# Attention and two feed-forward layers on one core: weights held split, six blocks of 384 tokens, attention's output stored as addends

## The chip, the core and the metric

The kernel runs on 1 core of a Trainium2 chip (8 cores; the other seven idle). The metric is the device time of one execution in microseconds (us), lower being better. TensorE is called PE here, VectorE DVE, ScalarE ACT, GpSimd POOL and SyncE SP. The kernel's DMAs are issued by SP, a few of them by ACT or POOL; an engine's DMA queue has a q behind its name (SPq, ACTq).

## The reference

Attention over 4 batches of 8 heads, 576 tokens and 64 columns a head, with rotary embedding; its output is x with 2304 tokens of 512 columns. Then two feed-forward layers ("MoE" in the names, but with one expert), from 512 to 2048 and back. q, k and v are float32; the weights are float64 and reach the kernel as pairs of 32-bit words, which it has to convert itself.

```python
q_rot, k_rot = rotate(q), rotate(k)
scores = scale * np.matmul(q_rot, k_rot.transpose(0, 1, 3, 2))
scores = scores - np.max(scores, axis=-1, keepdims=True)
attn = np.exp(scores)
attn = attn / (np.sum(attn, axis=-1, keepdims=True) + 1e-09)
x = np.matmul(attn, v)               # then to [2304, 512]
h = np.maximum(x @ w_in, 0.0)
x = h * h @ w_out                    # layer 0
h = x @ w_in2
g = np.maximum(h, 0.0) + alpha * np.minimum(h, 0.0)
out = g @ w_out2                     # layer 1
```

## The kernel before, in words

**Precision.** PE multiplies in fp32r, which keeps fewer bits than float32. Each factor is therefore split into a high part (a copy to fp32r) and a low part (the factor less its high part), and each product is three matmuls: high × high, high × low, low × high. A matmul here has a 128 × 128 stationary tile and streams up to 512 columns.

**Attention** (`attention`, L49) takes two heads at a time, 16 pairs. A pair has nine steps. `scores` (L190) does four or eight 288-column matmuls into PSUM, the row maximum on DVE (L208) and the exponential on ACT, which also sums the rows (L209). `trans` (L217) and `trans_tail` (L234), four steps later, transpose the exponentials on PE and split them on the way out of PSUM (L214 on ACT, L215 on DVE). `pv` (L250) multiplies with v in ten matmuls per half head. In a tile of `pv`, rows 0 to 63 belong to the high part of v and rows 64 to 127 to the low part, and the two halves have still to be added. `copy` (L125) brings it to SBUF as `st`. `outp` (L263) transposes `st` back (L280, L285: ten transposes a pair), adds the two halves (ACT L290, DVE L291) and multiplies by the reciprocal of the row sums on POOL (L292) into xn. After the four pairs of a batch, `xturn` (L294) transposes xn again (L300, 20 transposes a batch) and sends x to DRAM (L306). `turn` (L142) transposes the rotated q and k of the next pair, splits them (L148, L149) and stacks the parts by 18 DMAs on SP (L179). The rotary embedding (`rope`) runs on POOL.

Through attention the order on every engine is chosen by the framework's scheduler, which lets ready instructions pass others. After it, `manual_schedule` (L568) makes PE, DVE, ACT and POOL take program order.

**MoE** (`moe`, L396) has five blocks of tokens (`BLOCKS`, L388: 512, 256, 512, 512, 512). A layer takes block after block, and in each block 16 units of the first product (z = 0) and 16 of the second (z = 1). One unit uses one weight of 128 × 512 and has 12 matmuls. In layer 1's second product the weights are the streamed side, 512 columns for each 128 tokens. For a weight, `convert` (L421) loads the 64-bit words (L425) and takes them apart on DVE (L431 to L433), `power` (L436) forms the exponent on ACT, and `join` (L440) puts the sign in on DVE (L442) and multiplies mantissa and power on POOL (L444). The float32 weights are held. At each use, `prepare` (L460) splits the weight again with `split` (L447): the high part on ACT (L451), the low part on DVE or POOL (L452). That makes 320 splits. `prepare_x` (L468) loads a chunk of 128 columns of x for a block and splits it; `finish` (L509) applies the activation, in layer 0 a relu on ACT (L516) and the square on POOL (L525), or at the block's end copies the result out. The table `jobs` (L548) says ahead of which unit each weight is converted: layer 0's weights one a unit during the first block, layer 1's during the last block of layer 0 and the first of layer 1.

Of the kernel before, what the change touches and what calls it, by code (L numbers as in the profile page):

```python
# [9 lines left out]
F32 = mybir.dt.float32  # L10
# [17 lines left out]
NQ = 5  # L28
# [5 lines left out]
KQB, STB, XNB, PTB = 2, 4, 1, 3  # L34
RB = 2
# [3 lines left out]
XOE, STE = "A", "AAAA"  # L39
OP, OPD, OO, OX, OXD, OV = 0, 2, 3, 6, 2, 3  # L40


def col_base(b):

    g = (b // 2) * 2 * S
    return (g, g + 512) if b % 2 == 0 else (g + 640, g + 576)


def attention(tc, q, k, v, ident, ident_d, rope_d, xd, follow):  # L49
# [8 lines left out]
    with ExitStack() as at:  # L58
# [5 lines left out]
        sm = pool("asm", 2)  # L64
        kq = fpool("akq", KQB)
        nat = fpool("anat", 1)
        rp = fpool("arope", 1)
        ld = fpool("ald", 2)
        cp = fpool("acst", 1)
        ps_sc = fpool("ps_sc", NSC, space=PSUM)  # L70
# [13 lines left out]
        raw, rot = {}, {}  # L84

        def load(n, nm, heads=slice(0, 2), tail=None):
            b, hp = pairs[n]
            src = k if nm == "k" else q
            if (n, nm) not in raw:
                raw[n, nm] = ld.tile([P, 2, 5, D], F32, name=f"{nm}raw")  # L90
            m = raw[n, nm]
            hs = slice(2 * hp + heads.start, 2 * hp + heads.stop)
            nc.sync.dma_start(out=m[:, heads, 0:4].rearrange("p h r d -> p h (r d)"),
                              in_=src[b, hs, 0:512, :].rearrange("h (p r) d -> p h (r d)", r=4))
            for x in range(2):
                (tail or nc.sync).dma_start(out=m[64 * x:64 * x + 64, heads, 4],
                                            in_=src[b, hs, 512:576, :].rearrange("h p d -> p h d"))

        def load_v(n):
            b, hp = pairs[n]  # L100
            hs = slice(2 * hp, 2 * hp + 2)
            m = ld.tile([P, 2, NQ, D], F32, name="vraw")
            nc.sync.dma_start(out=m[:, :, 0:4].rearrange("p h r d -> p h (r d)"),
                              in_=v[b, hs, 0:512, :].rearrange("h (p r) d -> p h (r d)", r=4))
            for j in range(2):
                nc.sync.dma_start(out=m[64 * j:64 * j + 64, j, 4], in_=v[b, 2 * hp + j, 512:576, :])
                G.memset(m[64 - 64 * j:128 - 64 * j, j, 4], 0.0)
            raw[n, "v"] = m

        def rope(n, nm, c0=0, c1=NR, E=G):  # L110
            w = c1 - c0
            x = raw[n, nm].rearrange("p h r (t d) -> p (h r) t d", t=2)[:, c0:c1]
# [12 lines left out]
        def copy(out, in_, e):  # L125
            if e == "A":
                A.activation(out=out, in_=in_, func=AF.Copy)
            else:
                V.tensor_copy(out=out, in_=in_)

        vv, ops = {}, {}

        def vsplit(n):

            x = raw[n, "v"].rearrange("p h r d -> p (h r) d")
            t = sm.tile([P, 2, NQ, 2, D], F32R, name="vs", bufs=KQB)
# [51 lines left out]
        sums, Pt, PT, xn = {}, {}, {}, {}  # L188

        def scores(n, i, j):  # L190
            qT, kH, kL = ops[n]
            if (i, j) == (0, 0):
                sums[n] = sm.tile([P, 9], F32, name="sums", bufs=3)
# [8 lines left out]
            for y, (lhs, k0) in enumerate(prods):  # L202
                for kx, st in ((kH, True), (kL, False)):
                    for hf in range(2):
                        T.matmul(sc[:, hf, 0:SH], lhsT=lhs, rhs=kx[:, k0 + hf * SH:k0 + (hf + 1) * SH],  # L205
                                 start=st and y == 0, stop=not st and y == len(prods) - 1)
# [3 lines left out]
                         func=AF.Exp, bias=nm, accum_out=sums[n][:, 2 * i + j:2 * i + j + 1])  # L210
# [38 lines left out]

        def pv(n, j, hf, st):  # L250
# [3 lines left out]
            for c in range(NQ):  # L254
                for x in range(2):
                    t = PT[n, j][x][:, c, sl] if c < 4 else PT[n, "tail"][x][:, sl]
                    T.matmul(acc[:, 0:SH], lhsT=vs[:, j, c].rearrange("p a d -> p (a d)"), rhs=t,  # L257
                             start=(c == 0 and x == 0), stop=(c == 4 and x == 1))
            copy(st[:, sl], acc[:, 0:SH], STE[2 * j + hf])

        ris = {}

        def outp(n, j, sts):  # L263

            b, hp = pairs[n]
            if (hp, j) == (0, 0):
                xn[b] = sm.tile([P, NQ, DM], F32, name="xn", bufs=XNB)
            if j == 0:
                s, ri = sums[n], sm.tile([P, NQ, 2], F32, name="ri", bufs=3)
                rf = ri.rearrange("p i j -> p (i j)")  # L270
                V.tensor_scalar(s, s, 1e-9, None, ALU.add)
                V.reciprocal(rf[:, 0:9], s)
                V.tensor_copy(out=rf[0:64, 9:10], in_=rf[64:128, 8:9])
                ris[n] = ri
            ri = ris[n]
            u = ps_t.tile([P, 512], F32, name="ps", tag="t")
            if j < 2:
                rows, w, h = P, 4, 2 * hp + j
                for i in range(4):
# [363 lines left out]
```

## Time and profile before

| what | value |
|---|---|
| median of 3 runs | 1238.13 us (1237.96 to 1240.72) |
| profiled execution | 1237.75 us |
| its span, first to last instruction | 1235.9 us |
| mean granted TensorE clock | 0.992 of full speed |
| DMA traffic | 103.43 MB, mean 84 GB/s |
| busy: PE, DVE, ACT, POOL | 1131.9, 889.6, 706.6, 546.7 us |

A row of a view gives for each instruction group its line of the kernel (L205), its engine and operation, and the tiles it writes and reads (out<-in). What stands in brackets at a row's end is the idle time in front of it and what ended it. Busy times of different engines overlap; only a wait that ends last costs time. The kernel has stages one after the other (attention, layer 0, layer 1), and a mean over the span mixes them, so the table of stretches tells more than the shares of the whole.

### The profile page before, as it was taken

Reading aid. Unit: us, or ns where it says so; the run is one execution under the profiler, and the core shown is the slowest. Engines: PE = TensorE matmul, PEld = TensorE weight load, DVE = VectorE, ACT = ScalarE, POOL = GpSimd, SP = SyncE. Lnnn points to the kernel's source line nnn. Section 1 sums busy time; section 2 is a strip of 40 time slices with the busy share of each in tenths; the row PEclk is TensorE's granted clock in tenths of the full one; section 3 lists DMA queues with packets and bytes.
Section 4 is the critical chain, followed back from the end, with each engine's and each line's share of the span. In section 5 each row is a group of like instructions: output and inputs, shape, how many; then the busy total and the mean of one; then the engine's idle time right before and its main releaser. Section 6 shows DMA issues by size and latency. Waiting matters only on the chain.

```text
span 1235.9 us, 17781 instructions
## 1 busy us (share of the span) xinstructions
PE 1131.9 (92%) x6096; PEld 960.4 (78%) x6096; DVE 889.6 (72%) x1353; ACT 706.6 (57%) x1470; POOL 546.7 (44%) x493
## 2 busy tenths in 40 slices
PE   2799999999988766999999999998899999999998
PEld 1698989898876544898888887776689888888887
DVE  3688878788799999474544569999978665465453
ACT  1588888888875544574544454554456545445443
POOL 7667665764225465403104026556536250340430
PEclk9899999999999999999999999999999999999999
DMA  6656665756545434210010123342210101000100
GB/s 162 157 126 163 146 165 132 167 136 126 135 124 171 126 113 135 69 53 1 26 43 1 34 69 110 102 134 69 81 61 15 45 1 35 34 1 10 35 1 34
DMA packets 93496, 103.43 MB, mean 84 GB/s; under 512 B 29664, under 2 KB 68576, under 8 KB 93408
## 3 DMA queue, kind: packets, MB, share of 16 engines
q1 hardware_dynamic: 92720, 101.63, 30.7%
q8 instruction: 48, 0.79, 0.3%
q10 hardware_dynamic: 432, 0.56, 0.1%
q14 instruction: 40, 0.33, 0.1%
q0 software_dynamic: 256, 0.13, 0.0%
HBM read 58.76 MB, written 14.16 MB: 59 GB/s over the span
## 4 chain that ended last, share of the span: by engine, by line
PE 67%; DVE 12%; issue 7%; ACT 4%; POOL 4%; SPq 3%; DMA 2%; ACTq 0%; DVEq 0%; POOLq 0%
PE py L507 27%; PE ph L490 8%; PE ph L488 8%; PE ph L489 8%; PE sc L205 5%; PE acc L257 4%; PE ps L226 4%; ACT p L209 2%; SPq L179 2%; POOL w L444 2%; DVE pw L442 2%; DVE wl L452 2%; DVE man L433 2%; POOL wl L452 2%; DVE nm L208 1%
## 5 line engine op out<-in xcount | busy, mean ns | idle before, releaser
L452 DVE TENSOR_TENSOR wl<-w,wh 128x512 fp32r<-128x512 f32 x304 | 229.6, 756 | 96.4 <-ACT wh L451 92.1
L490 PE MATMUL ph<-xh,wl 128*128 128x512 f32 (+1 forms) x640 | 239.1, 374 | 19.1 <-DVE wl L452 19.0
L488 PE MATMUL ph<-xh,wh 128*128 128x512 f32 (+1 forms) x640 | 237.1, 371 | 3.0 <-ACT wh L451 2.9
L489 PE MATMUL ph<-xl,wh 128*128 128x512 f32 (+1 forms) x640 | 237.0, 370 | 0.0
L451 ACT ACTIVATE wh<-w 128x512 fp32r<-128x512 f32 x320 | 198.4, 620 | 25.8 <-POOL w L444 13.0
L521 POOL TENSOR_TENSOR g<-r,mn 128x512 f32<-128x512 f32 (+1 forms) x80 | 126.1, 1579 | 191.7 <-DVE mn L520 191.7
L452 DVE TENSOR_TENSOR gl<-g,gh 128x512 fp32r<-128x512 f32 (+1 forms) x160 | 121.2, 757 | 93.6 <-ACT gh L451 93.4
L516 ACT ACTIVATE r<-ph 128x512 f32<-128x512 f32 (+1 forms) x160 | 88.4, 553 | 160.3 <-PE ph L490 151.6
L444 POOL TENSOR_TENSOR w<-man,pw 128x512 f32<-128x512 f32 x64 | 110.1, 1721 | 156.3 <-DVE pw L442 149.7
L451 ACT ACTIVATE gh<-g 128x512 fp32r<-128x512 f32 (+1 forms) x160 | 93.8, 586 | 145.6 <-PE py L507 127.7
L490 PEld LDWEIGHTS ph<-xh,wl 128*128 128x128 f32 x640 | 121.5, 190 | 46.6 <-DVE wl L452 26.9
L507 PE MATMUL py<-gl,wh 128*128 128x512 f32 (+1 forms) x320 | 120.7, 377 | 25.5 <-DVE gl L452 25.5
L488 PEld LDWEIGHTS ph<-xh,wh 128*128 128x128 f32 x640 | 121.6, 190 | 23.6 <-ACT wh L451 4.0
L208 DVE TENSOR_REDUCE nm<-sc 128x1 f32<-128x576 f32 x144 | 107.9, 749 | 43.0 <-PE sc L205 43.0
L525 POOL TENSOR_TENSOR g<-r 128x512 f32<-128x512 f32 (+1 forms) x72 | 71.9, 998 | 150.7 <-ACT r L516 150.7
L489 PEld LDWEIGHTS ph<-xl,wh 128*128 128x128 f32 x640 | 121.3, 190 | 20.4
L209 ACT ACTIVATE p<-sc,nm 128x576 f32<-128x576 f32 x144 | 106.6, 742 | 27.3 <-DVE nm L208 26.0
L507 PE MATMUL py<-gh,wl 128*128 128x512 f32 (+1 forms) x320 | 118.8, 371 | 0.8 <-POOL wl L452 0.8
L507 PE MATMUL py<-gh,wh 128*128 128x512 f32 (+1 forms) x320 | 118.5, 370 | 0.0
L215 DVE TENSOR_TENSOR ptl<-ps,pth 128x512 fp32r<-128x512 f32 (+1 forms) x160 | 100.5, 633 | 22.5 <-ACT pth L214 20.6
L507 PE MATMUL py<-wh,gl 128*128 128x512 f32 x288 | 113.6, 394 | 2.7 <-DVE gl L452 2.6
L507 PE MATMUL py<-wl,gh 128*128 128x512 f32 x288 | 113.1, 393 | 1.7 <-DVE wl L452 1.7
(97 smaller groups left out, 2278.6 us busy)
## 6 DMA issues: line engine op xcount, KB each, us to landing
w<-in_moe_w_in_dram SPq DMA_DIRECT2D x32, 512.0 KB, 3.8
w<-in_moe_w_out_dram SPq DMA_DIRECT2D x32, 512.0 KB, 3.6
kH<-nath SPq DMA_DIRECT2D x64, 144.0 KB, 2.6
kL<-natl SPq DMA_DIRECT2D x64, 144.0 KB, 2.5
xr<-x SPq DMA_DIRECT2D x32, 256.0 KB, 2.7
vraw<-in_v_dram SPq DMA_DIRECT2D x16, 256.0 KB, 2.8
x<-y SPq DMA_DIRECT2D x16, 256.0 KB, 2.1
out_dram<-y SPq DMA_DIRECT2D x16, 256.0 KB, 2.3
```

Source lines behind the costliest of these rows:

```text
L208: V.tensor_reduce(out=nm, in_=sc[:, :, 0:SH], axis=AX.XY, op=ALU.max, negate=True)
L209: A.activation(out=Pt[n, i][:, j * S:(j + 1) * S].rearrange("p (a b) -> p a b", a=2), in_=sc[:, :, 0:SH], func=AF.Exp, bias=nm, accum_out= ...
L215: V.tensor_tensor(out=sl(lo), in0=src, in1=sl(hi).bitcast(F32), op=ALU.subtract)
L444: G.tensor_tensor(out=dst, in0=frac, in1=pw.bitcast(F32), op=ALU.mult)
L451: A.activation(out=hi[:, :w], in_=src, func=AF.Copy)
L452: lo_eng.tensor_tensor(out=lo[:, :w], in0=src, in1=hi[:, :w].bitcast(F32), op=ALU.subtract)
L488: T.matmul(ph[:, :w], lhsT=wh[:, cs], rhs=xh[:, :w], start=(c == 0), stop=False)
L489: T.matmul(ph[:, :w], lhsT=wh[:, cs], rhs=xl[:, :w], start=False, stop=False)
L490: T.matmul(ph[:, :w], lhsT=wl[:, cs], rhs=xh[:, :w], start=False, stop=(c == KC - 1))
L507: T.matmul(acc, lhsT=x, rhs=y, start=(s0 and k == 0), stop=(s1 and k == 2))
L516: A.activation(out=r[:, :w], in_=ph[:, :w], func=AF.Relu)
L521: G.tensor_tensor(out=g[:, :w], in0=r[:, :w], in1=mn[:, :w], op=ALU.add)
```

## The change

The weights of a layer are converted once and straight into their two fp32r parts, which are held in SBUF; the split at each use is gone.

- **Conversion** (class `Weights`) has the stages load, convert (three DVE operations, L380 to L382), grow (ACT, L387), sign (two DVE operations, L392 and L393) and join (two ACT copies, L399 and L400, and one POOL multiply, L401).
- **Blocks.** There are six blocks of 384 tokens. The first two blocks of layer 0 (`FIRST`) are taken together: each weight serves a unit of one and then a unit of the other. `EVERY0`, `EVERY1` and `EVERY2` say how many units apart the weights are converted.
- **Layer 1's weights** are converted during blocks 2 to 4 of layer 0 and their split form is written to DRAM (L447); `hold` (L453) loads it back during block 5, where a unit has used its slot for the last time.
- **Attention's output** is no longer transposed, added or divided in attention. `pv` sends the two halves to DRAM as they are (ACT's queue, L274), and `over` (new) sends the reciprocal row sums (L257, L258). `prepare_x` adds the halves (L496, DVE) and multiplies by the reciprocals (L497, POOL), which the DMA spreads over 64 partitions (L495). In the first two blocks there is one buffer for the addends (xr) and one for the reciprocals (r).
- **PE in attention** takes program order (`manual_schedule` on PE alone). The second part of step 8's scores is cut into 288, 224 and 64 columns.
- **Fewer DMA issues.** Two pairs are loaded at once, and the stacking of q and k takes 12 DMAs a pair instead of 18.

```diff
-KQB, STB, XNB, PTB = 2, 4, 1, 3
-RB = 2
+KQB, STB, PTB = 2, 2, 3
+RB = 1
...
+        front.enter_context(tc.manual_schedule(engines={mybir.EngineType.PE}))
...
+                for o, y, x, gap in ((kH, (0, 0), 0, 0), (qT, (0, 1), 1, 64), (kL, (1, 1), 0, 0)):
+                    for j in range(2):
+                        c0, o0 = 64 * (1 - j), j * (S + gap)
+                        for z in range(2):
+                            nc.sync.dma_start(out=o[64 * z:64 * z + 64, o0:o0 + S].bitcast(F32),
+                                              in_=f[64 * j:64 * j + 64, y[z], x, c0:c0 + S])
...
+        def over(n):
+
+            b, hp = pairs[n]
+            t = sums[n][:, 0:9]
+            V.tensor_scalar(t, t, 1e-9, None, ALU.add)
+            V.reciprocal(t, t)
+            u = ps_t.tile([P, 512], F32, name="ps", tag="t")
+            T.transpose(u[0:32, 0:P], sums[n], ident)
+            r = sm.tile([9, P], F32, name="ri")
+            A.activation(out=r, in_=u[0:9, 0:P], func=AF.Copy)
+            for j in range(2):
+                nc.scalar.dma_start(out=rd[hp, j, b * S:b * S + 512].rearrange("(i p) -> i p", i=4), in_=r[4 * j:4 * j + 4, :])
+            nc.scalar.dma_start(out=rd[hp:hp + 1, :, b * S + 512:b * S + 576], in_=r[8:9, :].rearrange("o (j c) -> o j c", j=2))
...
+            if hf == 0:
+                V.tensor_copy(out=st[j][:, sl], in_=acc[:, 0:SH])
+                return
+            A.activation(out=st[j][:, sl], in_=acc[:, 0:SH], func=AF.Copy)
+            b, hp = pairs[n]
+            nc.scalar.dma_start(out=xd[j, :, hp, b * S:(b + 1) * S], in_=st[j])
...
-BLOCKS = [(0, 512), (512, 256), (768, 512), (1280, 512), (1792, 512)]
+NB, W = 6, 384
+FIRST = 2
+STEPS_AHEAD, EARLY = 7, 2
+HELD0, OUT0 = 4, 10
+EVERY0, EVERY1, EVERY2 = 1.8, 2, 2.9
...
+        self.stages = ((-2, self.load), (0, self.convert), (1, self.grow), (2, self.sign), (3, self.join))
...
+    def convert(self, st, *j):
+        V = self.nc.vector
+        w64 = self.parts[j]
+        lo, hi = w64[:, :, 0], w64[:, :, 1]
+        m = st.tile([P, 512], U32, name="m", bufs=2)
+        V.tensor_scalar(m, hi, 0x1FF, None, ALU.bitwise_and)
+        V.scalar_tensor_tensor(out=m.bitcast(F32), in0=lo, scalar=2.0 ** -32, in1=m, op0=ALU.mult, op1=ALU.add)
+        V.tensor_scalar(lo, hi, 0x7FFFFE00, None, ALU.bitwise_and)
...
+        A.activation(out=lo.bitcast(F32), in_=lo.bitcast(F32), func=AF.Copy, scale=2.0 ** -20)
+        A.activation(out=wc[:, 0], in_=hi.bitcast(F32), func=AF.Copy)
+        G.tensor_tensor(out=wc[:, 1], in0=m.bitcast(F32), in1=lo.bitcast(F32), op=ALU.mult)
...
+            xr = xp[0].tile([P, 2, W], F32, name="xr", bufs=1 if first(layer, b) else 2)
+            x = xr[:, 0]
+            if layer == 0:
+                r = xp[0].tile([P, W], F32, name="r", bufs=1)
+                for j in range(2):
+                    nc.sync.dma_start(out=xr[64 * j:64 * j + 64],
+                                      in_=xd[j, :, c, c0:c0 + W].rearrange("(y d) c -> d y c", y=2))
+                    nc.sync.dma_start(out=r[64 * j:64 * j + 64], in_=rd[c, j:j + 1, c0:c0 + W].to_broadcast([D, W]))
+                V.tensor_tensor(out=x, in0=x, in1=xr[:, 1], op=ALU.add)
+                G.tensor_tensor(out=x, in0=x, in1=r, op=ALU.mult)
...
+                if (layer, b) == (0, NB - 1):
+                    hold(z, i)
```

How it moves instructions is seen in the order in which they stand on an engine. PE in the middle of attention, before: scores are L205, transposes of exponentials L226, products with v L257, output transposes L280 and xturn's L300, the next pair's q and k L154.

```order
L205 MATMUL sc<-kL,qT 128x288 x2
L226 MATMUL ps<-ident,p 128x128 x4
L300 MATMUL ps<-ident,xn 128x128 x4
L257 MATMUL acc<-pth,vs 128x288
...
L257 MATMUL acc<-pttl,vs 128x288
L154 MATMUL ps<-ident,rotk 128x128 x4
L205 MATMUL sc<-kH,qT 128x288 x2
L205 MATMUL sc<-kL,qT 128x288 x2
L226 MATMUL ps<-ident,p 128x128 x4
L280 MATMUL ps<-ident,st 128x128 x4
L205 MATMUL sc<-kH,qT 128x288 x2
```

The same place now (scores L201, transposes of exponentials L222, products with v L267):

```order
L201 MATMUL sc<-kH,qT_117 128x288 x2
L201 MATMUL sc<-kL,qT_117 128x288 x2
L222 MATMUL ps<-ident,p 128x128 x4
L267 MATMUL acc<-pth,vs 128x288
...
L267 MATMUL acc<-pttl,vs 128x288
L201 MATMUL sc<-kH,qT_117 128x288 x2
L201 MATMUL sc<-kL,qT_117 128x288 x2
L201 MATMUL sc<-kH,qT_117 128x288
L201 MATMUL sc<-kH,qT_117 128x224
L201 MATMUL sc<-kH,qT_117 128x64
```

Output transposes and xturn are gone, and the ten products of a half head stand together behind the two steps that the program puts before them. On ACT, five DMA issues a pair (L257, L258, L274) now stand between the exponentials (L205), the splits of the transposed ones (L210) and the copy of v's products (L272):

```order
L205 ACTIVATE p,sums<-sc,nm 128x576
L272 ACTIVATE st_1906<-acc 128x288
L274 DMA x_64<-st_1906 128x576
L143 ACTIVATE nat<-ps 128x512
L210 ACTIVATE pth<-ps 128x4x128
...
L255 ACTIVATE ri<-ps 9x128
L257 DMA r_65<-ri 4x128
L205 ACTIVATE p,sums<-sc,nm 128x576
...
L257 DMA r_65<-ri 4x128
L258 DMA r_65<-ri 2x1x64
```

Before, ACT issued no DMA there; an issue stands behind the copy that it sends, in the queue of the next exponential. SP at the end of attention, before: the chunks of x for the first two blocks (L471, xr) and the first weights' 64-bit words (L425, w64).

```order
L471 DMA xr_5364<-x1_64 128x512
L471 DMA xr_5370<-x1_64 128x512
L471 DMA xr_5376<-x1_64 128x512
L471 DMA xr_5382<-x1_64 128x512
L471 DMA xr_6207<-x1_64 128x256
L471 DMA xr_6244<-x1_64 128x256
L425 DMA w64_5388<-in_moe_w_in_dram 128x4x256
L425 DMA w64_5396<-in_moe_w_in_dram 128x4x256
```

SP there now (L493 the addends, L495 the reciprocals, L371 the weights' words); the first block's chunks 2 and 3 and the second block's chunks 0 and 1:

```order
L371 DMA w64_4773<-in_moe_w_in_dram 128x4x256
L493 DMA xr_4751<-x1_64 64x2x384 x2
L371 DMA w64_4799<-in_moe_w_in_dram 128x4x256
L371 DMA w64_4828<-in_moe_w_in_dram 128x4x256
L495 DMA r_4764<-r1_65 64x384 x2
L493 DMA xr_4763<-x1_64 64x2x384 x2
L371 DMA w64_4841<-in_moe_w_in_dram 128x4x256
L371 DMA w64_4867<-in_moe_w_in_dram 128x4x256
L495 DMA r_4776<-r1_65 64x384
L493 DMA xr_4775<-x1_64 64x2x384 x2
L371 DMA w64_4887<-in_moe_w_in_dram 128x4x256
L495 DMA r_4786<-r1_65 64x384 x2
```

A chunk is four DMAs instead of one, and loads of weights stand between the chunks, where before the first block's chunks stood ahead of all weights. There are three buffers of w64, so from the fourth weight on a load waits until an earlier weight is joined.

## Rows read from the trace of the kernel before

**Rows 1.** The profile page: busy times; GB/s in 40 slices of the span.

```profile
PE 1131.9 (92%) x6096; PEld 960.4 (78%) x6096; DVE 889.6 (72%) x1353; ACT 706.6 (57%) x1470; POOL 546.7 (44%) x493
...
GB/s 162 157 126 163 146 165 132 167 136 126 135 124 171 126 113 135 69 53 1 26 43 1 34 69 110 102 134 69 81 61 15 45 1 35 34 1 10 35 1 34
```

**Rows 2.** Stretches: their length, each engine's busy time, clock, DMA share, GB/s.

```profile
203.00:223.00 20.00, 18.88 (x146) 17.63 (x145) 16.70 (x32) 16.56 (x42) 13.86 (x17) 1.00 0.65 147
366.00:506.00 140.00, 103.76 (x419) 76.10 (x420) 131.81 (x159) 66.78 (x120) 79.10 (x58) 0.98 0.43 133
386.00:396.00 10.00, 7.47 (x24) 5.05 (x23) 7.51 (x9) 4.72 (x8) 7.02 (x6) 0.83 0.35 109
366.00:553.00 187.00, 150.76 (x806) 122.88 (x807) 162.28 (x211) 100.29 (x193) 88.94 (x74) 0.98 0.36 111
553.00:822.00 269.00, 263.75 (x1149) 216.11 (x1149) 174.20 (x226) 131.00 (x231) 88.68 (x65) 0.99 0.18 54
822.00:1232.00 410.00, 399.29 (x1827) 329.73 (x1825) 273.61 (x393) 201.72 (x370) 153.71 (x95) 1.00 0.11 35
```

**Rows 3.** PE's timeline: start, duration, instruction; first and last pair, hand-over.

```profile
58.54 0.42 PE L244 MATMUL ps<-ident,p 128*64 128x128 f32 x1
...
351.87 0.43 PE L205 MATMUL sc<-kL,qT 128*128 128x288 f32 x2
...
360.36 0.27 PE L244 MATMUL ps<-ident,p 128*64 128x128 f32 x1
...
366.01 0.50 PE L488 MATMUL ph<-xh,wh 128*128 128x512 f32 x1 [1.42 <-ACT wh L451]
```

**Rows 4.** The chain that ended last, in order of time: start, duration, instructions.

```profile
202.95 0.87 PE ps L226 x8
...
208.18 1.07 PE sc L205 x8
...
529.46 23.29 PE py L507 x192
...
1188.52 43.53 PE py L507 x192
```

**Rows 5.** Groups by line and form: count, busy us, mean ns, idle before.

```profile
L127 ACT ACTIVATE st<-acc 128x288 f32<-128x288 f32 x64 | 26.4, 413 | 4.0 <-PE acc L257 4.0
L290 ACT ACTIVATE oa<-ps 128x256 f32<-128x256 f32 x32 | 12.2, 382 | 3.0 <-PE ps L280 3.0
L475 DVE TENSOR_TENSOR xl<-xr,xh 128x512 fp32r<-128x512 f32 x32 | 21.9, 683 | 0.1
L475 DVE TENSOR_TENSOR xl<-xr,xh 128x256 fp32r<-128x256 f32 x8 | 3.3, 411 | 0.0
L525 POOL TENSOR_TENSOR g<-r 128x512 f32<-128x512 f32 x56 | 62.0, 1108 | 132.2 <-ACT r L516 132.2
L525 POOL TENSOR_TENSOR g<-r 128x256 f32<-128x256 f32 x16 | 9.8, 615 | 18.5 <-ACT r L516 18.5
```

**Rows 6.** Timelines of ACT's and SP's DMA queue: start, duration of the issue.

```profile
1.18 0.45 ACTq L316 DMA_DIRECT2D ident<-in_c_ident_dram  x1
...
327.67 0.59 SPq L179 DMA_DIRECT2D qT<-nath  x1
```

**Rows 7.** The page's DMA issues: count, KB each, us from issue to landing.

```profile
xr<-x SPq DMA_DIRECT2D x8, 128.0 KB, 2.3
```

**Rows 8.** DVE's timeline over two weights of the first block.

```profile
402.15 0.68 DVE L452 TENSOR_TENSOR wl<-w,wh 128x512 fp32r<-128x512 f32 x1
...
403.36 0.41 DVE L431 TENSOR_SCALAR man<-w 128x512 uint32<-128x512 uint32 x1
403.69 1.52 DVE L432 TENSOR_SCALAR pw<-w 128x512 uint32<-128x512 uint32 x1
405.13 0.68 DVE L433 SCALAR_TENSOR_TENSOR man<-w,man 128x512 f32<-128x512 uint32 x1
...
410.16 0.68 DVE L452 TENSOR_TENSOR wl<-w,wh 128x512 fp32r<-128x512 f32 x1
```

**Rows 9.** POOL's timeline in the same stretch.

```profile
403.51 1.42 POOL L444 TENSOR_TENSOR w<-man,pw 128x512 f32<-128x512 f32 x1 [1.83 <-DVE pw L442]
```

More of the change, by code (lines that the diff above doesn't have):

```diff
@@ L38, with attention @@
 OP0, OPD0, OP1, OPD1 = 2, 2, 0, 2
[L39 to L49, printed above, removed]
+OP, OPD, OV = 0, 2, 3
+def attention(tc, q, k, v, ident, ident_d, rope_d, xd, rd, follow):
     nc = tc.nc
@@ L99, in load_v @@
[L99 to L108, printed above, removed]
+        rot = {}
@@ L447, in split @@
-        def split(src, w, tag, lo_eng):
-            sp = wp if tag == "w" else late["sp"]
-            hi = sp.tile([P, 512], F32R, name=f"{tag}h")
-            lo = sp.tile([P, 512], F32R, name=f"{tag}l")
-            A.activation(out=hi[:, :w], in_=src, func=AF.Copy)
-            lo_eng.tensor_tensor(out=lo[:, :w], in0=src, in1=hi[:, :w].bitcast(F32), op=ALU.subtract)
-            return hi, lo
-        units = [(layer, b, z, i) for layer in range(2) for b in range(len(BLOCKS)) for z in range(2) for i in range(FC)]
@@ L456, in moe @@
[L456 to L475 removed]
+        XW = FIRST * W
@@ new lines, in moe, with slot @@
+        units = [(0, b, z, i) for z in range(2) for i in range(FC) for b in range(FIRST)]
+        units += [(layer, b, z, i) for layer in range(2) for b in range(0 if layer else FIRST, NB)
+                  for z in range(2) for i in range(FC)]
+        NU = len(units)
+        at_unit = {u: t for t, u in enumerate(units)}
+        ws, kept, gt, gsp, xsp, hs, accs, late = {}, {}, {}, {}, {}, {}, {}, {}
+        def slot(z, i):
+            p = (held0 if i < HELD0 else late["held1"]) if z == 0 else late["out0" if i < OUT0 else "out1"]
+            return p.tile([P, 2, 512], F32R, name="w")
@@ new lines, in first, with hidden, split_g @@
+        def first(layer, b):
+            return layer == 0 and b < FIRST
+        def hidden(layer, b, i):
+            if first(layer, b):
+                k, c0 = (0, 0, i), b * W
+            else:
+                k, c0 = (layer, b, i // 2), i % 2 * W
+            if k not in gt:
+                gt[k] = late["g1" if k[:2] == (0, 0) and i < FC // 2 else "g0"].tile([P, XW], F32, name="g")
+            return gt[k][:, c0:c0 + W]
+        def split_g(u):
+            layer, b, z, i = units[u]
+            if z == 0:
+                return
+            g = hidden(layer, b, i)
+            hi = late["sp"].tile([P, W], F32R, name="gh")
+            lo = late["sp"].tile([P, W], F32R, name="gl")
+            A.activation(out=hi, in_=g, func=AF.Copy)
+            V.tensor_tensor(out=lo, in0=g, in1=hi.bitcast(F32), op=ALU.subtract)
+            gsp[u] = hi, lo
@@ L571, in moe @@
             if 0 <= t + 1 < NU:
[L572 to L575 removed]
+                split_g(t + 1)
             unfinished += [t - 1] if 0 <= t - 1 < NU else []
@@ L579, in moe @@
                     finish(unfinished.pop(0))
+            if t == at_unit[0, 0, 1, 0]:
+                xfirst.close()
+                xp[0] = pool("xp1", KC, side="right")
+                late["wc"] = pool("wc", 2, side="right")
+            if t == at_unit[0, FIRST - 1, 1, FC // 2 - 1]:
+                gfirst.close()
+                late["out1"] = pool("out1", FC - OUT0)
+            for d, stage, j in sorted(jobs.get(t, []), key=lambda x: x[0]):
+                stage(st, *j)
             if 0 <= t < NU:
                 layer, b, z, i = units[t]
-                nxt = (layer, b + 1) if b + 1 < len(BLOCKS) else (layer + 1, 0)
-                if z == 1 and 4 <= i < 4 + KC and nxt[0] < 2:
+                if (layer, b) == (0, NB - 1):
+                    hold(z, i)
+                nxt = (layer, b + 1) if b + 1 < NB else (layer + 1, 0)
+                if z == 1 and 4 <= i < 4 + KC and nxt[0] < 2 and not first(*nxt):
                     prepare_x(*nxt, i - 4)
```

418 lines of the change are left out of this document (187 added, 231 removed).

## The prediction, as it was put on record

> **What bounds the kernel now.** The page first [rows 1]: PE is busy for 92% of the span, so only PE work that goes, or a stall of PE, is worth much. The profiled execution took 1237.75 us over a span of 1235.9; I make the sum against it. The median of the three runs, 1238.13, is 0.4 above it; a measurement can tell about 0.3% (3.7 us) from no change.
>
> Then the table of stretches [rows 2], which the PE timeline's marks cut [rows 3]. Attention: from the L244 transpose of the first pair (58.54) to that of the last (360.36) there are 15 pairs in 301.8 us, 20.1 each; in 203 to 223 PE works 18.88 us of 20, DVE 16.70, ACT 16.56, POOL 13.86. No engine is full: chains between them end last, and PE waits some 2 us a pair. Hand-over: last scores at 352.3, when attention's right-hand buffers come free, first MoE matmul at 366.0, 13.7 later. First two blocks (768 tokens), 366 to 553: DVE is busy 132 us of the first 140 and PE only 104. Rest of layer 0, 553 to 822, and layer 1, 822 to 1232: PE is busy for 264 of 269 and 399 of 410, so little more than matmul time is there.
>
> The chain gives that time [rows 4]: a transpose 0.109 us, a 288-column matmul 0.133, one of 256 columns 23.29/192 = 0.121, of 512 43.53/192 = 0.227. A straight line puts 384 columns at 0.173. A unit of 12 such matmuls is 2.08 us, so columns cost the same in blocks of 384; only stalls and empty columns can be won in MoE.
>
> **The sum, part by part.**
>
> *Attention.* Gone per pair: 10 output transposes (L280, L285) and on average 5 of xturn, 15 × 0.109 = 1.6 us; new: one transpose of the sums and two 64-column matmuls, 0.3. PE's work falls from about 18.1 to 16.5. ACT loses three oa copies (0.38 + 0.38 + some 0.3 by columns) and half of its four 0.41 us copies of sums to DVE [rows 5], and xturn's: about 2 less. It gains a small copy and five DMA issues, at 0.45 each [rows 6] 2.25. ACT so ends near 17.2 and is now the longest queue. DVE loses two-source adds, gains two copies and stays near 16; POOL loses the multiplies. Before, PE's 18.1 came out at 20.1, nine tenths; 17.2 at a like share is 18.5. Bounds: 17.1, if program order leaves no chain open, and 19.9, the plain pairs of now. Fifteen pairs × 1.6 = **−24**. Twelve stacking DMAs instead of 18, at 0.6 on SP [rows 6], come in the first turn with no cover: **−4** (0 to −8). The last scores so fall near 324.
>
> *Hand-over.* The chunks of x for the first two blocks go through one xr and one r buffer. A chunk is two more issues of 0.6, a landing of 2.3 [rows 7], an add and the low part on DVE at 0.55 each, a high copy on ACT at 0.5 and a multiply on POOL at 0.86 (between the 256- and 512-element rows [rows 5]); some wait between engines is in it: 5.2 to 6.1 us, eight times in series. What is late next: SP has weight loads in front of chunk 2, and in front of the second block's chunks loads that wait for a w64 buffer, so for the first weights' conversions. The second block's four chunks stand ready near 43 us after the last scores. PE's order alternates the two blocks, so until then it can do units 0 and 2 and parts of 1 and 3, 8.3 us in all; matmuls run in earnest as if from 36.7, against 13.7 now: +23. After an idle stretch the clock is low: 0.83 in 386 to 396 [rows 2], where a stall had gone before. Some 2 us more: **+25**. Bounds: 0 if the chunks land under the end of attention, +30 if PE can do nothing before all are there.
>
> *First 768 tokens.* Now 187. Then 64 units × 2.08 = 133, and stalls. Converting a weight now is five DVE operations (three at 0.41 and two at 0.68 when nothing else is in the way, 2.6) and a POOL multiply (1.4), but the split at each use is gone, and one weight serves two units. The cycle of now does two weights in 8.0 us [rows 8], 0.92 of the durations added up (8.66), so I take the new cycle in the same way: 2.63 + 1.33 + two g splits of 0.55 = 5.1, × 0.92 = 4.7 us a weight against 4.16 of PE. That is 0.5 × 16 in the second half, and as much for the next block's x and for weights that come late in the first: 16. Total 149, **−38**; bounds 133 and 175.
>
> *Rest of layer 0.* Now 269. Then 128 units, 266, and about 12 of stalls: layer 1's conversions are spread over blocks 2 to 4, one every 2.9 units, under PE's 6.0 us, but each block's next x goes through one r buffer, 3.7 us of chunk work at least against units of 2.08. 278: **+9**; bounds 266 and 290. In block 5 SP reloads 32 split weights of 0.5 MB, 16.8 MB in 66.6 us, 252 GB/s; 366 to 506 moves 133 at a DMA share of 0.43 [rows 2], so 309 at a full one, and I cost the reload at nothing; its cover is the matmuls of block 5. At 171, the most that a slice of the page shows [rows 1], it would take 98 us, and the last weight would still land before layer 1's 32nd unit wants it, 131 us after the start of block 5: its bound is 0 too, and only x, which waits in the same queue, could be some us late.
>
> *Layer 1.* Now 410 with conversion in it [rows 2]. Then 96 × 12 × 0.173 + 96 × 9 × 0.227 = 396 and 2 for stalls: **−12**; bounds 396 and 415. In its place DVE and ACT have only g and mn to do. The tail after the last matmul stays: three stores of 128 rows, cut at the batch borders, as now 0.
>
> Sum: −24 − 4 + 25 − 38 + 9 − 12 = −44, so **1194 us**.
>
> **Rivals.**
>
> *A. ACT's queue closes attention (slower).* PE takes instructions in program order, and ACT issues five DMAs a pair between exponentials; a wait of one stands in front of the next exponential, then of transposes, then of PE, which may not step past them. For it: ACT has 83% of 203 to 223 now. Against: it is work of some 17 us. If a pair costs 23, where PE's 16.5, with the 2 us that PE waits now, has another 4.5 of ACT's issues and copies in series, that is 2.9 × 15 = +44 where I had −24: 1194 + 68 = 1262. It decides from a pair of 20.1 + (1238 − 1194 − 24)/15 = 21.4 on. Chance 0.07.
>
> *B. DVE and POOL lock each other.* For it [rows 8, 9]: L432, one read and one write, takes 1.52 us at 403.69 while POOL multiplies from 403.51 to 404.93, where the same kind of operation (L431) takes 0.41 before it. If each weight's DVE and POOL work goes strictly in series, a weight is 2.6 + 1.4 + two g splits (1.1) + half a square (0.4) = 5.5 us; 28 weights in the stretch are 154, with the x chunks some 175 instead of 149, and chunks in the blocks after cost 10 more: 1194 + 36 = 1230. Against it: the cycle of now has the two overlap by a little (0.92). Chance 0.12. The Trainium skill, SBUF — State Buffer, section "Who interferes with whom", states that DVE and GpSimd share one pair of ports as an exclusive lock, taken also by tensor_scalar in its two-port modes and, for reads, by operations with two SBUF inputs, and that the loser is fully blocked. By that rule the time is this rival's, 1230; the trace agrees for L432 (1.52 beside 0.41).
>
> *C. The x chunks are hidden.* If SP and POOL get the first chunks done before the last scores (their batches are long finished by then), the hand-over is no longer than now: 1194 − 25 = 1169. Against: their buffers lie where attention's are, and wait for weights stands in SP's queue. *D. Attention near PE's floor*, 17 us a pair, is −22 more: 1172. C and D together 0.22.
>
> *E. Attention's pair stays.* If chains from scores to exponentials to transposes set the pair, and not a full engine, fewer operations win nothing, and program order loses what the scheduler's stepping past had won: 19.9 a pair, so −3 instead of −24: 1215. For it: no engine of 203 to 223 is over 94%, and the plain pairs of now run at just that. Chance 0.14.
>
> **Numbers.** My forecast 0.41, A 0.07, B 0.12, C and D 0.22, E 0.14, others 0.04. The range goes from C or D with a stall or two fewer (1156) to B (1230); A, the upper side of B and C with D together lie outside, some 0.18. Faster by over 0.3% (under 1234) are the forecast, C, D, E and most of B: 0.87. B's upper end gives 0.04 within 0.3%; slower are A and half of the others: 0.09.
>
> **What would show it.** Pairs 18.5 us apart at the sums' transposes, with ACT the longest queue; 36 to 44 us between the last scores and the stretch where PE is full, and waits on DMA xr and POOL x there; no PE idle over 1 us in layer 1; L381 and L382 of two durations, near 0.7 or 0.4 and near 1.5, the long ones beside POOL. A pair over 21 us, or PE idle in more than a fifth of the first 150 us of MoE, would make the forecast wrong.

## The result, and the profile after

The changed kernel takes 1252.89 us (median of 4 runs, 1249.85 to 1254.82) against 1238.05 of the kernel before beside it: a ratio of 1.0114, 95% interval 1.0088 to 1.0140. It is slower by 1.1%, where 1194 and a range of 1156 to 1230 were forecast. The profiled run took 1252.51 us.

The page, and the stretches of the changed kernel that answer to [rows 1, 2] (columns as there): attention, from the last scores to near the eighth chunk of x, the rest of the first two blocks, blocks 2 to 5, layer 1.

```profile
PE 1118.2 (89%) x6480; PEld 1047.9 (84%) x6480; DVE 690.5 (55%) x1179; ACT 603.4 (48%) x1292; POOL 440.4 (35%) x404
```

```profile
203.00:223.00 20.00, 18.75 (x151) 18.12 (x150) 17.63 (x32) 15.73 (x40) 13.49 (x12) 1.00 0.53 134
318.00:375.00 57.00, 28.19 (x122) 22.71 (x121) 27.91 (x52) 17.53 (x37) 10.54 (x10) 0.71 0.48 139
375.00:540.00 165.00, 136.94 (x725) 128.74 (x726) 120.10 (x181) 92.15 (x172) 59.52 (x49) 0.97 0.39 117
541.00:849.00 308.00, 284.72 (x1536) 275.66 (x1535) 158.02 (x261) 147.57 (x280) 83.42 (x76) 0.96 0.59 189
849.00:1245.00 396.00, 395.82 (x2016) 361.55 (x2014) 125.89 (x219) 111.42 (x224) 100.33 (x96) 1.00 0.08 24
```

DVE, ACT and POOL all work less than before, and so does PE, yet the kernel is longer: every engine waits more. The marks that cut it, from views of single lines (count: shortest/median/longest ns, first and last start): the transposes of the sums, one a pair; block 2's first matmuls; the last z = 1 matmuls of layer 0.

```profile
L253 PE MATMUL ps<-ident,sums x16: 269/284/415, 51.6 to 329.8; 128*32 128x128 f32 x16
```

```profile
L511 PE MATMUL ph<-xh,w x4: 334/334/334, 540.3 to 541.9; 128*128 128x384 f32 x4
```

```profile
L529 PE MATMUL py<-gh,w x640: 331/334/690, 450.7 to 848.6; 128*128 128x384 f32 x160
```

A pair takes (329.8 − 51.6)/15 = 18.55 us, as forecast. The last scores end at 318.3, the last matmul of all at 1244.7. So:

| stretch | forecast us | measured us | off by |
|---|---|---|---|
| start to last scores | 324 | 318.3 | −6 |
| last scores to block 2 (hand-over 38.7, first two blocks 149) | 188 | 222.0 | +34 |
| blocks 2 to 5 | 278 | 308.7 | +31 |
| layer 1 | 398 | 395.7 | −2 |
| behind the last matmul | 4 | 6 | +2 |

Three places lose it. In the rows xh and xl are the high and the low part of a chunk of x, gh and gl those of the second product's input g.

**Hand-over**: PE's waits after the last scores.

```profile
345.14 0.69 PE L511 MATMUL ph<-xh,w 128*128 128x384 f32 x1 [3.28 <-ACT xh L500]
353.82 0.69 PE L511 MATMUL ph<-xh,w 128*128 128x384 f32 x1 [7.08 <-ACT xh L500]
360.96 0.62 PE L511 MATMUL ph<-xh,w 128*128 128x384 f32 x2 [1.39 <-ACT xh L500]
368.19 0.69 PE L511 MATMUL ph<-xh,w 128*128 128x384 f32 x1 [5.68 <-ACT xh L500]
375.31 0.69 PE L511 MATMUL ph<-xh,w 128*128 128x384 f32 x1 [4.56 <-ACT xh L500]
```

The last four chunks come 7.2 us apart (5.2 to 6.1 forecast), the eighth 57 us after the last scores (43). One round on SP's queue, and DVE's two operations in it:

```profile
354.50 1.25 SPq L493 DMA_DIRECT2D xr<-x  x2
360.38 1.11 SPq L495 DMA_DIRECT2D r<-r  x2
361.60 1.26 SPq L493 DMA_DIRECT2D xr<-x  x2
```

```profile
358.67 0.56 DVE L496 TENSOR_TENSOR xr<-xr 128x384 f32<-128x384 f32 x1 [4.31 <-DMA xr<-x]
360.94 0.56 DVE L501 TENSOR_TENSOR xl<-xr,xh 128x384 fp32r<-128x384 f32 x1 [1.71 <-ACT xh L500]
```

From 354.50 to 361.60 the chain is the two issues of the addends (1.25 us), 2.9 us to the add (358.67 − 354.50 − 1.25), and 2.9 us from the add through POOL's multiply (359.36, 0.99), ACT's high copy and DVE's low part to the next issue. The reciprocals' two issues (360.38) run beside the high copy and the low part.

**Conversion beside the second product of the first two blocks**, one weight on DVE, on POOL and on ACT:

```profile
521.06 0.56 DVE L477 TENSOR_TENSOR gl<-g,gh 128x384 fp32r<-128x384 f32 x1 [0.81 <-ACT gh L476]
...
522.60 0.42 DVE L380 TENSOR_SCALAR m<-w 128x512 uint32<-128x512 uint32 x1
523.05 0.69 DVE L381 SCALAR_TENSOR_TENSOR m<-w,m 128x512 f32<-128x512 uint32 x1
523.78 1.51 DVE L382 TENSOR_SCALAR w<-w 128x512 uint32<-128x512 uint32 x1
525.21 0.55 DVE L477 TENSOR_TENSOR gl<-g,gh 128x384 fp32r<-128x384 f32 x1
```

```profile
518.19 1.30 POOL L401 TENSOR_TENSOR w<-m,w 128x512 fp32r<-128x512 f32 x1 [4.20 <-ACT w L399]
523.69 1.31 POOL L401 TENSOR_TENSOR w<-m,w 128x512 fp32r<-128x512 f32 x1 [4.21 <-ACT w L399]
```

```profile
525.37 0.76 ACT L387 ACTIVATE w<-w,pbias 128x512 uint32<-128x512 uint32 x1 [1.20 <-POOL w L401]
526.03 0.51 ACT L476 ACTIVATE gh<-g 128x384 fp32r<-128x384 f32 x1
```

POOL's multiplies start 5.5 us apart (4.7 forecast, 4.16 is PE's work), and L382 lasts 1.51 beside one, where L380, the same kind of operation, takes 0.42. DVE's own work in a round, from 521.06 to the end of the row at 525.21, is 4.7 us. Then DVE stands 0.8 us for the next gh. On ACT that gh is behind L387, which works on what L382 has written and starts 0.08 us after L382's end (the row names POOL, which was done before, at 525.00).

**Chunks of x for later blocks**, one of them on DVE, POOL, ACT and PE in turn:

```profile
583.76 1.68 DVE L381 SCALAR_TENSOR_TENSOR m<-w,m 128x512 f32<-128x512 uint32 x1
...
585.82 0.55 DVE L496 TENSOR_TENSOR xr<-xr 128x384 f32<-128x384 f32 x1
```

```profile
583.50 1.39 POOL L401 TENSOR_TENSOR w<-m,w 128x512 fp32r<-128x512 f32 x1 [5.00 <-ACT w L399]
...
586.45 0.99 POOL L497 TENSOR_TENSOR xr<-xr,r 128x384 f32<-128x384 f32 x1 [1.56 <-DVE xr L496]
591.42 0.99 POOL L497 TENSOR_TENSOR xr<-xr,r 128x384 f32<-128x384 f32 x1 [3.98 <-DMA r<-r]
```

```profile
587.47 0.52 ACT L500 ACTIVATE xh<-xr 128x384 fp32r<-128x384 f32 x1 [3.54 <-POOL xr L497]
587.90 0.51 ACT L476 ACTIVATE gh<-g 128x384 fp32r<-128x384 f32 x1
```

```profile
588.46 0.45 PE L529 MATMUL py<-gh,w 128*128 128x384 f32 x1 [2.06 <-ACT gh L476]
```

ACT waits 3.54 us for a chunk that nobody needs before the next block; behind it, in program order, stands gh, which PE needs now. Four units take some 5 us each here, instead of 2.08, before each of blocks 2 to 5, and three of these places lie in the stretch of blocks 2 to 5.

### The profile page after: what moved, and what is told of

It reads as the page before. It is cut to its first block, busy times and chain, and to the rows that moved or that the text cites. A ratio compares the mean times of both kernels' runs of the same rounds, so it can differ in the third digit from the quotient of the medians.

```text
span 1250.7 us, 18130 instructions
## 1 busy us (share of the span) xinstructions
PE 1118.2 (89%) x6480; PEld 1047.9 (84%) x6480; DVE 690.5 (55%) x1179; ACT 603.4 (48%) x1292; POOL 440.4 (35%) x404
## 4 chain that ended last, share of the span: by engine, by line
PE 61%; DVE 12%; POOL 8%; DMA 8%; issue 5%; ACT 5%; SPq 2%; ACTq 0%; POOLq 0%; DVEq 0%
PE py L529 24%; PE ph L511 9%; PE ph L512 9%; PE ph L513 9%; PE acc L267 3%; PE sc L201 3%; PE ps L222 2%; DVE m L381 2%; POOL xr L497 2%; DMA kraw<-in_k_dram 2%; DMA r<-r 2%; POOL w L401 2%; DMA xr<-x 2%; DVE w L382 1%; DVE ptl L211 1%
## 5 line engine op out<-in xcount | busy, mean ns | idle before, releaser
L511 PE MATMUL ph<-xh,w 128*128 128x384 f32 x768 | 260.4, 339 | 29.4 <-ACT xh L500 22.0
L512 PE MATMUL ph<-xl,w 128*128 128x384 f32 x768 | 259.5, 338 | 0.0
L513 PE MATMUL ph<-xh,w 128*128 128x384 f32 x768 | 258.7, 337 | 0.6 <-POOL w L401 0.6
L477 DVE TENSOR_TENSOR gl<-g,gh 128x384 fp32r<-128x384 f32 x192 | 109.7, 572 | 206.5 <-ACT gh L476 206.5
L529 PE MATMUL py<-gh,w 128*128 128x384 f32 x640 | 178.6, 353 | 23.7 <-ACT gh L476 23.7
L529 PE MATMUL py<-w,gh 128*128 128x512 f32 x576 | 177.4, 389 | 0.0
L511 PEld LDWEIGHTS ph<-xh,w 128*128 128x128 f32 x768 | 145.8, 190 | 33.8 <-ACT xh L500 24.0
L529 PEld LDWEIGHTS py<-gh,w 128*128 128x128 f32 x640 | 124.2, 200 | 28.3 <-ACT gh L476 28.3
L512 PEld LDWEIGHTS ph<-xl,w 128*128 128x128 f32 x768 | 145.7, 190 | 1.7 <-DVE xl L501 1.5
L513 PEld LDWEIGHTS ph<-xh,w 128*128 128x128 f32 x768 | 145.8, 190 | 0.9 <-POOL w L401 0.9
L401 POOL TENSOR_TENSOR w<-m,w 128x512 fp32r<-128x512 f32 x64 | 87.9, 1374 | 155.0 <-ACT w L399 136.0
L529 PEld LDWEIGHTS py<-w,gh 128*128 128x128 f32 x576 | 108.0, 188 | 22.2
L529 PE MATMUL py<-gl,w 128*128 128x384 f32 x320 | 115.5, 361 | 9.8 <-DVE gl L477 9.7
L205 ACT ACTIVATE p<-sc,nm 128x576 f32<-128x576 f32 x144 | 106.6, 741 | 25.7 <-DVE nm L204 18.9
L529 PE MATMUL py<-w,gl 128*128 128x512 f32 x288 | 112.2, 389 | 0.0
L210 ACT ACTIVATE pth<-ps 128x512 fp32r<-128x512 f32 (+1 forms) x160 | 86.9, 554 | 40.8 <-PE ps L222 40.1
```

Of the source, the lines that this page charges most:

```text
L205: A.activation(out=Pt[n, i][:, j * S:(j + 1) * S].rearrange("p (a b) -> p a b", a=2), in_=sc[:, :, 0:SH], func=AF.Exp, bias=nm, accum_out= ...
L401: G.tensor_tensor(out=wc[:, 1], in0=m.bitcast(F32), in1=lo.bitcast(F32), op=ALU.mult)
L477: V.tensor_tensor(out=lo, in0=g, in1=hi.bitcast(F32), op=ALU.subtract)
L511: T.matmul(ph[:, :W], lhsT=wh[:, cs], rhs=xh, start=(c == 0), stop=False)
L512: T.matmul(ph[:, :W], lhsT=wh[:, cs], rhs=xl, start=False, stop=False)
L513: T.matmul(ph[:, :W], lhsT=wl[:, cs], rhs=xh, start=False, stop=(c == KC - 1))
```

## The experiments

Theory X: program order on DVE, ACT and POOL makes chunks of x stop PE. Theory L (rival B of the prediction): POOL's multiply blocks DVE's conversion. Theory P (near rivals A and E): PE's program order or ACT's queue in attention. Differences below are between medians, from the changed kernel's 1252.89.

**e1**, the reciprocals' second buffer after the first two blocks.

```diff
-r = xp[0].tile([P, W], F32, name="r", bufs=1)
+r = xp[0].tile([P, W], F32, name="r", bufs=1 if first(layer, b) else 2)
```

> Edit: a second buffer for the reciprocals (r) in the blocks after the first two. Theory X (the chunks of x in program order: the landing of r starts only when the multiply before it has read the buffer, and the next unit's high part of g stands behind the chunk on ACT): a chunk that took about 5 us of a step drops to about 3.3, 16 chunks, so 25 us less than the changed kernel (about 1228). Theory L (the DVE/GpSimd lock sets the pace everywhere): under 4 us of difference. Theory P (program order on PE in attention costs): no difference.

Measured: 1246.46, only 6.4 less. DMA waits go (POOL's 3.98 in the second chunk's place is 2.17, on DVE), but the chain does not: another chunk of the same preparation,

```profile
601.45 0.52 ACT L500 ACTIVATE xh<-xr 128x384 fp32r<-128x384 f32 x1 [3.66 <-POOL xr L497]
```

still keeps ACT for 3.66 us. So the buffer is not the cause; the chain DVE, POOL, ACT ahead of gh is.

**e2**, chunks spread over the second product's 16 units (and e1's buffer).

```diff
-if z == 1 and 4 <= i < 4 + KC and nxt[0] < 2 and not first(*nxt):
-    prepare_x(*nxt, i - 4)
+if z == 1 and nxt[0] < 2 and not first(*nxt):
+    for f, d in ((load_x, 0), (scale_x, 3), (split_x, 4)):
+        if (i - d) % 3 == 0 and 0 <= (i - d) // 3 < KC:
+            f(*nxt, (i - d) // 3)
```

> Edit: as e1, and the four chunks of the next block are spread over the 16 units of the second product, loaded three units before they are added and multiplied, and split one unit after that, so that no engine meets a chunk that is not there. Theory X: the stalls of four preparations, some 11 us each, go: 45 us less than the changed kernel (about 1208), and PE is full from unit to unit in blocks 2 to 5. Theory L: at most 10 less, the stalls stay where conversions are. Theory P: nothing.

Measured: 1220.23, 32.7 less, where 45 were expected; ratio to the kernel before 0.9857 (0.9843 to 0.9872). Blocks 2 to 5 take 281 us (534.4 to 815.4) instead of 308, near the 278 forecast, and the stretch ahead of them 6 us less. A window of them, and all of PE's waits in them (L545 and L478 are L529 and L477 of the changed kernel):

```profile
537.00:816.00 279.00, 268.24 (x1526) 263.70 (x1526) 161.61 (x257) 147.42 (x280) 86.33 (x76) 1.00 0.65 206
```

```profile
PE py L545 <- DVE gl L478: 10.8, 11, 1.2
```

No wait for gh is left, as X says; some for gl are, where conversions are. And the stalls had cost twice: in the changed kernel PE was busy for 284.72 us of this stretch at a granted clock of 0.96, here for 268.24 at 1.00 in a window that has 10 matmuls fewer (under 2 us): some 15 us. Beside e1's buffer the edit does two things: it loads the chunks three units ahead and it takes their operations apart. The runs do not show what each is worth.

**e3**, the scheduler orders PE in attention.

```diff
-front.enter_context(tc.manual_schedule(engines={mybir.EngineType.PE}))
```

> Edit: PE's program order in attention undone; the scheduler orders PE there as before. Theory X and my prediction: ACT's queue sets the pair, so 18.5 us a pair stay within 0.3 and the time within 5 us. Theory P: pairs of 17 us and a time 20 us less. The other way round (program order is what brought the pairs down): pairs near 19.9 and 20 us more.

Measured: 1256.54, 3.6 more. Pairs are (328.5 − 55.4)/15 = 18.2 us, but the first sums come 3.8 us later. In the runs of this section that leave attention as it is, pairs lie between 18.31 and 18.55 and the first sums between 51.6 and 55.1, so little of either is e3's. Program order is neither the gain nor the loss.

**e4**, the joining multiply on DVE.

```diff
-G.tensor_tensor(out=wc[:, 1], in0=m.bitcast(F32), in1=lo.bitcast(F32), op=ALU.mult)
+V.tensor_tensor(out=wc[:, 1], in0=m.bitcast(F32), in1=lo.bitcast(F32), op=ALU.mult)
```

> Edit: the multiply that joins a weight's low part runs on DVE instead of POOL, so no POOL multiply stands beside DVE's conversion (POOL keeps squares and x). Theory L: L381 and L382 keep their short durations (0.7 and 0.43), a weight of the second product of the first two blocks takes about 4.7 us instead of 5.5, and the kernel 15 to 25 us less. Theory X: the chunks set the pace, conversions matter in the second product of the first two blocks alone: 5 to 15 us less, and the stalls of blocks 2 to 4 stay as they are.

Measured: 1231.67, 21.2 less, as L says; ratio to the kernel before 0.9942 (0.9921 to 0.9964). Groups of lines (count, busy us, mean ns, idle before), first of the changed kernel, then of e4:

```profile
L381 DVE SCALAR_TENSOR_TENSOR m<-w,m 128x512 f32<-128x512 uint32 x64 | 63.1, 987 | 2.2
L382 DVE TENSOR_SCALAR w<-w 128x512 uint32<-128x512 uint32 x64 | 44.2, 691 | 2.1
```

```profile
L401 DVE TENSOR_TENSOR w<-m,w 128x512 fp32r<-128x512 f32 x64 | 46.8, 731 | 29.8 <-ACT w L399 29.7
L381 DVE SCALAR_TENSOR_TENSOR m<-w,m 128x512 f32<-128x512 uint32 x64 | 48.7, 760 | 2.2
L382 DVE TENSOR_SCALAR w<-w 128x512 uint32<-128x512 uint32 x64 | 29.3, 457 | 2.0
```

A multiply that took POOL 1.37 us in the mean takes DVE 0.73, and L381 and L382 run at nearly their own time. DVE works 17.5 us longer in all (46.8 for the multiplies, 29.3 less for these two lines), so its load is not the gain. The round is: in the second product of the first two blocks a weight takes 4.39 us instead of 5.5,

```profile
499.57 0.68 DVE L401 TENSOR_TENSOR w<-m,w 128x512 fp32r<-128x512 f32 x1
503.96 0.69 DVE L401 TENSOR_TENSOR w<-m,w 128x512 fp32r<-128x512 f32 x1
```

since the 1.09 us that L382 had been held are gone, and the multiply stands where DVE waited for gh (0.18 us of that wait are left). 19.5 of the 21.2 us fall between the last scores and block 2 (202.5 us for 222.0), 8.8 of them in this second product (80.8 us for 89.6) and the rest before it. The chunk stalls stay: PE still waits 21.4 us for gh in the second product (23.7).

**e5**, two buffers for the first two blocks' chunks.

```diff
-xr = xp[0].tile([P, 2, W], F32, name="xr", bufs=1 if first(layer, b) else 2)
+xr = xp[0].tile([P, 2, W], F32, name="xr", bufs=2)
...
-r = xp[0].tile([P, W], F32, name="r", bufs=1)
+r = xp[0].tile([P, W], F32, name="r", bufs=2 if first(layer, b) else 1)
...
-late.update(held1=pool("held1", FC - HELD0), sp=pool("sp", 2), tp=pool("tp", 2), out0=pool("out0", OUT0),
+late.update(held1=pool("held1", FC - HELD0), sp=pool("sp", 2), out0=pool("out0", OUT0),
...
+if t == at_unit[1, 0, 0, 0]:
+    wcs.close()
+    late["tp"] = pool("tp", 2, side="right")
```

> Edit: a second buffer for xr and for r in the first two blocks (the space comes from the tile mn, which is allocated only when layer 1 starts). Theory X (the eight chunks go one after the other through one buffer, 7.2 us each in the changed kernel): chunks of the second block come about 4 us apart, the last matmul that waits for a chunk starts near 355 instead of 375, and the kernel takes some 20 us less (about 1233). If the weights' conversions were what holds the hand-over anyway: waits on the chunks turn into waits on weights and the time falls by under 6 us.

Measured: 1225.97, 26.9 less. The chunks come before the weights now: PE's last wait for a chunk is one of 0.33 us at 351.17 (375.31 in the changed kernel), and its longest wait behind the last scores is for a weight:

```profile
341.60 0.69 PE L513 MATMUL ph<-xh,w 128*128 128x384 f32 x1 [2.50 <-POOL w L401]
```

Some 4 us of the gain are of another kind. In the changed kernel PE waits 5.17 us at 328.46 for attention's last splits, which on DVE stand behind the first weight's conversion and the 4.93 us that this waits for its load (326.65); in e5 the scheduler has another order there, and that wait is 1.13.

**e6**, e2 with e4, and **e7**, e2, e4 and e5 together; the diffs are theirs.

> Edit: e2 and e4 together (chunks spread, and the joining multiply on DVE). If chunk stalls and the lock are two separate causes: 33 + 21 = 54 us less than the changed kernel, about 1200. If e4's gain was in the same stalls (conversions beside chunks): about 1212, 8 less than e2.

> Edit: e6 and e5 together. If the hand-over's chunks are a third separate cause: 18 to 22 us less than e6, about 1180. If DVE, which now has all of the conversion, becomes the bound of the first two blocks: under 10 less.

Measured: 1197.68, 55.2 less (33 + 21 = 54), and 1171.14, 81.8 less (33 + 21 + 27 = 81). The causes add, so they are three. e7 stands to the kernel before at 0.9468 (0.9453 to 0.9483) and is the fastest of all. Its stretches from the last scores on:

```profile
322.00:496.00 174.00, 155.62 (x860) 147.97 (x859) 146.92 (x267) 111.28 (x210) 26.42 (x26) 0.97 0.53 158
497.00:770.00 273.00, 267.39 (x1519) 262.73 (x1519) 169.15 (x288) 147.10 (x279) 41.08 (x44) 1.00 0.66 210
770.00:1166.00 396.00, 396.00 (x2019) 361.98 (x2017) 125.53 (x219) 111.53 (x224) 100.39 (x96) 1.00 0.09 25
```

**e8**, e4's edit in the kernel before (L444 on DVE).

> Edit of the kernel before: its joining multiply (L444) on DVE instead of POOL. Theory L (POOL's reads keep DVE's conversion from running): L432 and L433 fall from 1.24 and 1.08 us in the mean to about 0.45 and 0.7, two weights take about 6.2 us instead of 8.0 in spite of the added 0.6 each, and the kernel before gets 25 to 35 us faster (about 1208). If the long durations are the operations' own: DVE, which is the bound there, only gets longer, by 0.6 x 64, and the kernel 15 to 30 us slower.

Measured: 1219.10, ratio 0.9854 (0.9838 to 0.9871): 18.2 faster than the kernel before beside it, less than expected, but by the same mechanism; the multiply took DVE 0.96 us in the mean, where 0.6 were expected. L432 and L433, before and then in e8:

```profile
L432 DVE TENSOR_SCALAR pw<-w 128x512 uint32<-128x512 uint32 x64 | 79.6, 1244 | 0.0
L433 DVE SCALAR_TENSOR_TENSOR man<-w,man 128x512 f32<-128x512 uint32 x64 | 68.8, 1075 | 0.0
```

```profile
L433 DVE SCALAR_TENSOR_TENSOR man<-w,man 128x512 f32<-128x512 uint32 x64 | 44.1, 689 | 0.0
L432 DVE TENSOR_SCALAR pw<-w 128x512 uint32<-128x512 uint32 x64 | 29.1, 455 | 0.0
```

**e9**, attention's outputs sent by SP; the diff shows one of the three lines, the two on rd are changed alike.

```diff
-nc.scalar.dma_start(out=xd[j, :, hp, b * S:(b + 1) * S], in_=st[j])
+nc.sync.dma_start(out=xd[j, :, hp, b * S:(b + 1) * S], in_=st[j])
```

> Edit of the changed kernel: the five DMA issues a pair that send attention's output go through SP instead of ACT. By my prediction's model (ACT with its issues is the longest queue and sets the pair): pairs fall from 18.55 to about 17, and the time by some 20 us. By the other reading (PE, DVE and ACT are all near nine tenths and the chain between them sets the pair): pairs within 0.4 of 18.55, and the time within 6 us.

Measured: 1247.03, 5.9 less; pairs (323.6 − 53.9)/15 = 17.98, 0.57 shorter, not 1.5. Against the shortest pairs of the runs that leave attention as it is, 18.31, it is 0.33. So ACT's issues cost between a fifth and two fifths of what a model with ACT as the bound says.

**e10**, e7 with e9.

> Edit: e7 and e9 together. If the four causes add: 6 us less than e7, about 1165. If SP, which issues x's chunks and weights at the hand-over behind attention's last outputs, delays them: equal to e7 or slower.

Measured: 1180.04, 8.9 more than e7. Attention ends earlier as in e9 (last scores at 318.2, in e7 at 322.2), but at the hand-over SP has the chunks' DMAs, the weights' and attention's last outputs in one queue, and from the last scores to block 2 it takes 183.6 us, in e7 171.9. PE waits there for weights (7.8 us) and for chunks (3.6 us) now, longest (L527 is L511 of the changed kernel):

```profile
344.61 0.69 PE L527 MATMUL ph<-xh,w 128*128 128x384 f32 x1 [4.65 <-ACT w L401]
```

## Why the prediction was wrong

Three terms of the sum failed: the size of a chunk at the hand-over, the 4.7 us a weight of the first 768 tokens, which had no wait in it, and the 12 us of stalls in the rest of layer 0. Term by term:

- *Attention, −28*: right in size (−34: some 23 from the pairs, as forecast, 7 from the start, the rest in the last pair), but not by its model. ACT was not the longest queue: it worked 15.73 us of 20 in 203 to 223, DVE 17.63 and PE 18.75. Its five issues, which that number leaves out, took 1.84 us there (0.35 + 0.34 + 0.27 + 0.28 + 0.60, not 5 × 0.45), so with them it has at most 17.6, and taking them away gave 0.3 to 0.6 a pair (e9). Program order gave nothing (e3). By its own row PE worked 18.88 of 20 us before, 19.0 a pair and not 18.1; now it is 17.4. PE's share stays at 94%, and the pair fell by what PE's work fell. That speaks for PE's fewer instructions, but the runs did not try them alone.
- *Hand-over, +25*: the mechanism was right, one buffer and chunks in series, and the chunk was too short: 7.2 us for at most 6.1, so that the eighth comes 14 us later than the step had it. It put a landing of 2.3 us from a DMA of 128 KB, where the add came 2.9 us after the last issue, the multiply at 0.86 (0.99), and left some 0.1 for the starts from engine to engine (0.3). e5 prices the single buffers at 27, but the sum had 25 for this hand-over already.
- *First 768 tokens, 149*: some 20 us too short. A weight of the second product took 5.5 us and not 4.7: the step added durations up, scaled them by 0.92 and put no wait. DVE's own work did come to 4.7, the lock in it (L382 1.09 us longer beside 1.31 of POOL); what the step lacked is the 0.8 us in each round for which DVE stood for a gh that ACT does only behind L387, and so behind L382. The second product took 89.6 us (450.7 to 540.3) where its 32 units are 66.6; e4 takes 8.8 off it, and e2, by the chunks of block 2, 5. e4's other gain, 10.7, lies before it, in the hand-over and the first product, where the runs do not show which rounds it came from. That 0.92 fitted DVE's work is partly luck: 8.66 is what DVE's ten operations at 0.69 and 0.42 and POOL's two multiplies come to, and leaves out POOL's square in the same cycle (408.47, 1.22), beside which L433 took 1.52. Rival B said 5.5 us a weight, and 5.5 it was, also partly by luck: 0.4 of it is half a square, and POOL squares nothing in these rounds, where the wait of 0.8 stands instead. e4 prices the lock at 21. The Trainium skill, SBUF — State Buffer, section "Who interferes with whom", has the rule that the loser of DVE's and GpSimd's shared ports is fully blocked; the trace agrees but for some 0.14 us: L381 begins at 583.76, within POOL's multiply of 583.50 to 584.89, and ends 0.55 us behind it, where alone it takes 0.69.
- *Rest of layer 0, 278*: this is the largest miss, 31. The step compared 3.7 us of chunk work with units of 2.08 and put 12 us of stalls for all blocks. It was some 3 us for each of four units, three times in this stretch, since each chunk stood in front of the next unit's gh in ACT's order; and behind the stalls the clock was lower, which no term of this stretch had. e2 took 27 away here and e1 only 6, so the order of the work and its early load count, not the buffer that the step named.
- *Reload of the weights, 0*, and *layer 1, 398*: right (395.7).
- *Rivals*: A, C, D and E did not come. B's lock came, and alone, at B's 1230, would have given a faster kernel; the loss took it together with two terms that were too small.

## What to carry to other kernels

Where engines take program order, work for later must not stand in front of work for now: load, combine and split it in separate steps, far enough apart that each finds its input there (e2, 33 us for no operation saved). Work moved to a slower idle engine is not free if the busy engine stops for it: look for one line with two durations, and see what runs beside the long one. And an engine's durations added up give a round only if nothing in it waits for another engine: 4.7 us of DVE's work made rounds of 5.5.

## What the runs showed of the hardware

A stall of 2 to 3 us on PE costs more than itself. Blocks 2, 3 and 4 of the changed kernel have four waits for gh each (19.2 us in all, the longest 2.9), and their granted clocks are 0.96, 0.92 and 0.96, so part of the time it stood at the lower of its two levels, 1.2 GHz for 2.4; block 5, without such waits, has 1.00. Block 3:

```profile
620.70:702.80 82.10, 74.39 (x386) 71.29 (x385) 50.60 (x83) 43.20 (x82) 26.83 (x24) 0.92 0.56 183
```

Over blocks 2 to 5 PE was busy some 15 us longer than in e2 for the same matmuls, more than half of the 27 us between the two stretches. The reload of 32 split weights (16.8 MB) beside the matmuls of block 5 left PE without a wait, at 295 GB/s in its best 20 us:

```profile
820.00:840.00 20.00, 20.00 (x117) 20.00 (x117) 7.55 (x14) 6.92 (x14) 0.00 (x0) 1.00 0.88 295
```
